# Normalizing the attention output after its repacking, two blocks at a time

## The chip, the cores and the metric

One core of a Trainium2 chip runs the whole computation. The metric is device time in microseconds of one execution. The engines of the core work side by side[...]: TensorE (PE, matrix products and their weight loads), ScalarE (ACT, activation functions), VectorE (DVE), GpSimd (POOL), and SyncE (SP), which here only issues DMAs. Products land in PSUM, eight banks of 128 partitions by 512 float32; everything else lies in SBUF.

## The reference

Two layers of the same kind, each an attention part and a mixer and MLP part, on x of 1 x 2048 x 512 in bfloat16:

```python
def _A_ref(x, wq, wk, wv, wo):                    # H = 32 heads, Dh = 16
    q = (x @ wq).reshape(B, S, H, Dh).transpose(0, 2, 1, 3)
    k, v = x @ wk, x @ wv                         # one key and value head for all
    p = _softmax(einsum("bhqd,bkd->bhqk", q, k) * Dh ** -0.5)
    return einsum("bhqk,bkd->bhqd", p, v).transpose(0, 2, 1, 3).reshape(B, S, H * Dh) @ wo

x = x + _A_ref(_layernorm(x), A_wq, A_wk, A_wv, A_wo)
x = x + _B_ref(_layernorm(x), B_w1, B_w2, B_w3, B_w4)
# and both once more
```

`_B_ref` is a gelu projection with shifts along the sequence (w1, w2) and a gelu MLP of width 1792 (w3, w4), each behind a layernorm. The attention has no mask. The softmax needs a division by the row sum of the exponentials; where that division takes place is what the change is about.

## The kernel before

**The planner.** The program is not written as an order of instructions. `Plan` holds operations, each with its engine, the tags it reads and writes, a priority (lower goes first) and a duration, and plays them through in a model of the engines. The order that comes out is emitted, one instruction stream for each engine, with semaphore waits where an operation depends on one of another engine. So a stream is fixed when the program is built: on the chip an engine takes its instructions in that order and waits when one is not yet allowed. Durations in the code (`dur=`) only shape the plan.

**Attention.** The 2048 queries are cut into chunks (`CHUNKS`): four of 512 in layer 0; three of 512 and two of 256 in layer 1. A block is four heads of a chunk, so a chunk has eight blocks, 72 in all. A block's keys are passed in steps of 128 (two steps at once in the chunks of 256), each step in two halves of two heads. There are 2048 such halves. Each half's exponential is made in one of two ways:

- a *unit* (`declare_unit`): scores on PE, one exponential of 128 x 1024 on ACT (L1125) into EA, one group of value products on PE (L1230);
- a *pair* (`declare_pair`): scores of each head on PE into a bank of its own, two DVE instructions (L1143) that turn them into the bit pattern of an approximate exponential in J, two shifted copies of it made by `shift_op` (L1180, on POOL, or on DVE when POOL's queue holds `ADDS` or more), and three groups of value products, with the value copies in VD that are scaled for the three.

Units are made in order. `assign` is asked whenever scores are placed and turns a half that lies ahead into a pair, when fewer than `MAX_PAIRS` pairs are in flight, when DVE's queue is short and when its due side work is below `BACKLOG`. In the stage between the layers (layer 1's first chunk, keys before step 11, which are ready early) these two numbers are replaced by `CALM`, and in the last chunk by `CALM_END`. `TEMPER` is a string of one letter for each 12.5 us of planned time, which picks one of 16 sets of the planner's numbers, `MAX_PAIRS` and `ADDS` among them.

Beside the attention of one chunk runs the side work of the chunk before: output projection, mixer, MLP, and for layer 1 its normalized input, keys and values. `PACE` and priorities hold it back or push it.

**Layer 1's first chunk** is special. Its last keys come from layer 0's last chunk, so seven of its blocks are first done for keys 0 to 5, then 6 to 10, with partial sums spilled in between, and finished later (`end == "add"`), in short blocks of five key steps.

**The end of a block** (`block_end`) is where the change is. The value products of four heads lie in one PSUM bank, `ACC`: head x on partitions 32x to 32x+15, the sums of its exponentials on partition 32x+16. Before the change the steps are, for a block of n queries:

1. DVE copies ACC to ACCF (L1264, or L1260 with the spilled part added). ACCF holds 1024 columns: two blocks of 512, or four of 256. The next block's products wait for this copy.
2. PE turns the sums into columns (SELC, L1274), DVE takes reciprocals into RZ (L1281).
3. PE spreads the reciprocals over 128 x n in a PSUM bank, with RZ columns as weights against the identity (`fx`, L1289).
4. DVE multiplies ACCF by it into OS (L1295).
5. SP issues eight DMAs (L1318) that repack OS into half of an OT tile: row 64 (b mod 2) onwards of tile b // 2, with no gaps between heads. In the last chunk of a layer, blocks of number `LATE_OT` and over are repacked by PE and DVE instead (SELO, L1308, L1314).

When all eight blocks of a chunk are through, `chunk_end` declares the output projection from OT (L676 with WO, OT) and the sum into X (L1450).

Of the kernel before, what the change touches and what calls it, by code (L numbers as in the profile page):

```python
# [10 lines left out]
ALU = mybir.AluOpType  # L11
# [498 lines left out]
def t_ps(n):  # L510
    return 0.066 + n * 1.043e-3
# [14 lines left out]
def tiled(n, k=1):  # L526
    return ("P", n * k, n * k, range(4))
# [6 lines left out]
class Kernel:  # L534
# [16 lines left out]
    PARTS = (0.3203125, 0.25390625, 0.201171875)  # L551
    FILL = True
    HOLD = 0.1
    CALM = (1, 1)
    CALM_END = (2, 1)
    LATE_OT = 5
    PORTION = 2
    QUICK = -1
    PACE = ((2.8, 2.8, 2.2, 0.3), (2.8, 2.2, 0.5, 0.5, None))
# [29 lines left out]
    )  # L589
    TEMPER = "090ee27f7f97f71e3eee4ee77f547c4fe941e77e7385715f85317197105502005897e0e10e0ef77f27f593f70f1f030e1e77ee0975325855000003"  # L590

    def __init__(self, nc, ins, out):
        self.stretch = -1
# [22 lines left out]
    def memory(self):  # L616
        self.sbytes = 0
        sb = self.sb
        self.X = sb("X", [16, 512])
        self.IDENT = sb("IDENT", [128])  # L620
        self.ONES = sb("ONES", [512])
        self.NIL = sb("NIL", [128])
        self.SELC = sb("SELC", [4])
        self.SELO = sb("SELO", [2, 32])
        self.WQ = sb("WQ", [4, 528])
        self.WK = sb("WK", [4, 32])
        self.WV = sb("WV", [4, 32])
        self.WO = sb("WO", [4, 512])
        self.W1 = sb("W1", [4, 512])
        self.W2 = sb("W2", [4, 512])  # L630
        self.W3 = sb("W3", [4, 1792])
        self.W4 = sb("W4", [14, 512])
        self.KT = sb("KT", [2, 2048])
        self.VP = sb("VP", [2, 16, 32])
        self.VD = sb("VD", [3, 2, 16, 32])
        self.QT = sb("QT", [2, 8, 512])
        self.OT = sb("OT", [4, 512])
        self.OS = sb("OS", [1024])
        self.QS = sb("QS", [4, 512])
# [12 lines left out]
        self.RZ = sb("RZ", [32])  # L652
        self.OUTB = sb("OUTB", [2, 512])
        self.ST6 = sb("ST6", [16, 6], dt.float32)
        self.MV = sb("MV", [16, 2], dt.float32)
        self.SM = sb("SM", [4, 16], dt.float32)
        self.MH = sb("MH", [2, 16], dt.float32)
        assert self.sbytes <= 208 * 1024, self.sbytes / 1024
        pb = self.stack.enter_context(self.nc.psum_tensor("PB", [128, 8, 512], dt.float32))
        self.PB = pb[:, :, :]  # L660
        self.PBH = self.shaped(pb[:].rearrange("p a b -> p (a b)").bitcast(dt.bfloat16), [8, 1024])
        kt0 = self.KT[:, 0, :].bitcast(dt.float32)
        ob = self.OUTB.rearrange("p a b -> p (a b)").bitcast(dt.float32)
# [46 lines left out]
    def head(self):  # L710
        pl = self.pl
        op = pl.op
        ins = self.ins
# [14 lines left out]
        def fill(eng, ap, v, tags, dur, prio):  # L728
            op(eng, lambda e: e.memset(ap, v), writes=tags, dur=dur, prio=prio)
# [36 lines left out]
        self.qproj(0, 0, prio=3, blocks=(1,), direct=True, after=[("KT", 0, 7)])  # L766
        self.qproj(0, 0, prio=3, blocks=range(2, 8), after=[("KT", 0, 7)])
        fill("POOL", self.SELC, 0.0, [("SELC",)], 0.1, 3)
        op("POOL", lambda e: e.affine_select(out=self.SELC, in_=self.SELC, compare_op=ALU.not_equal,
                                             fill=1.0, base=-16, pattern=[[-32, 4]],  # L770
                                             channel_multiplier=1),
# [247 lines left out]
    def make_groups(self):  # L1019
# [47 lines left out]
        self.pairs = []  # L1067
        self.adds = []
        self.fin_left = {}
        self.main_done = False  # L1070

    def inputs(self, g):
# [165 lines left out]
    def block_end(self, la, c, b, end):  # L1238
        op = self.pl.op
# [10 lines left out]
            return  # L1250
        n = self.size(la, c)
        nq = n // 128
        m = self.nfin % (1024 // n)
        self.nfin += 1
        parts = range(2 * m, 2 * m + 2) if n == 512 else (m,)
        am, zm, om = ([(x, i) for i in parts] for x in ("ACCF", "RZ", "OS"))
        acc, rz, osm = self.ACCF[:, m * n:m * n + n], self.RZ[:, 4 * nq * m:4 * nq * (m + 1)], self.OS[:, m * n:m * n + n]
        if end == "add":
            ap, tags = self.SPILL[b]
            self.last_copy = op("DVE", lambda e: e.tensor_tensor(  # L1260
# [2 lines left out]
        else:  # L1263
            self.last_copy = op("DVE", lambda e: e.tensor_copy(acc, self.PB[:, self.ACC, 0:n]),  # L1264
               writes=[("AC",)] + am, dur=t_ps(n), prio=0, side=False)
        fin = min(5, self.RUSH[la][c])
        L = Late()

        def fz(e):
# [8 lines left out]

        def frec(e):
            with self.nc.allow_low_precision("the reciprocals feed a bf16 matmul"):  # L1280
                return e.reciprocal(rz, self.PB[:, L.bank, 0:4 * nq])  # L1281
        op("DVE", frec, writes=[L] + zm, dur=0.17, prio=fin, give=L)
        M = Late()
        for h in range(nq // 2):
            def fx(e, h=h):
                ins = None
                for q in (2 * h, 2 * h + 1):
                    for g in range(4):
                        ins = e.matmul(self.PB[32 * g:32 * g + 32, M.bank, q * 128:(q + 1) * 128],  # L1289
                                       lhsT=rz[:, 4 * q + g:4 * q + g + 1].to_broadcast([128, 32]),  # L1290
                                       rhs=self.IDENT, start=True, stop=True, tile_position=(0, 32 * g))
                return ins
            op("PE", fx, reads=zm + [("ID",)], writes=[M], pe=("P", 256, 256, range(4)), prio=fin,
               take=M if h == 0 else None)
        op("DVE", lambda e: e.tensor_tensor(out=osm, in0=acc, in1=self.PB[:, M.bank, 0:n],  # L1295
                                            op=ALU.mult),
           reads=am, writes=[M] + om, dur=t_ps(n), prio=fin, give=M)
        r0 = 64 * (b % 2)
        hw = n // 2
        if c == len(self.CHUNKS[la]) - 1 and b >= self.LATE_OT:  # L1300
            N = Late()

            def fo(e):
                ins = None
                for u in range(2):
                    for p in range(2):
                        x = r0 + 32 * p
                        ins = e.matmul(self.PB[x:x + 32, N.bank, u * hw:u * hw + hw], lhsT=self.SELO[:, u, :],  # L1308
                                       rhs=osm[:, p * hw:p * hw + hw], start=True, stop=True,
                                       tile_position=(0, x), skip_group_check=True)  # L1310
                return ins
            op("PE", fo, reads=om + [("SELO", i, u) for i in range(2) for u in range(2)], writes=[N],
               pe=("P", 2 * hw, hw, (r0 // 32, r0 // 32 + 1)), prio=fin, take=N)
            op("DVE", lambda e: e.tensor_copy(self.OT[r0:r0 + 64, b // 2, 0:n], self.PB[r0:r0 + 64, N.bank, 0:n]),  # L1314
               writes=[N, ("OT", b)], dur=t_ps(n), prio=fin, give=N)
        else:
            op("SP", lambda e: [
                e.dma_start(self.OT[r0 + 16 * (2 * p + i):r0 + 16 * (2 * p + i) + 16, b // 2, u * hw:u * hw + hw],  # L1318
                            osm[32 * (2 * i + u):32 * (2 * i + u) + 16, p * hw:p * hw + hw])
                for p in range(2) for i in range(2) for u in range(2)],  # L1320
               reads=om, writes=[("OT", b)], dma=128 * n, parts=8, prio=fin)
        if end == "add" and b >= 3:
            self.qproj(1, 1, prio=11, blocks=(2 * b - 6, 2 * b - 5), direct=True)
            if b == self.SPILLED - 1:
# [2 lines left out]
        left.discard(b)  # L1327
        if not left:
            self.chunk_end(la, c)

    def temper(self, now):
        w = int(now / self.STRETCH)
# [307 lines left out]
```

## Time and profile before

| what | value |
|---|---|
| three runs | 1483.88, 1484.53, 1486.28 us; median 1484.53 |
| the profiled execution | 1481.02 us, span 1479.2 us |
| granted TensorE clock, mean | 0.999 |
| value copies to ACCF | 65 plain (49 of 512, 16 of 256), 7 with the spilled part |
| multiplies into OS | 72: 56 of 512 at 680 ns, 16 of 256 at 413 ns |
| reciprocals | 72: 248 ns (512), 199 ns (256) |
| OT casts of the matmul repack | 6: 687 ns (512), 424 ns (256) |
| OT DMAs | 424 of 8 KB, 1.8 us to landing, and 104 of 4 KB, 2.2 us |
| filler products (ONES, NIL) | 532 matmuls, 49 us |

The span is the time from the first to the last instruction that the profiler saw. A busy PE is not a PE at its peak, since its instructions overlap and their ends are modelled[...]. Waits name the instruction that released the waiting one. The chain of waits is followed back from the last instruction of the program: an engine with a large share of it sets the time.

### The profile page before, as it was taken

The numbers are of one execution on the slowest core, as the hardware profiler recorded it, in microseconds if no ns is written. First come the engines' busy times: TensorE is split into PE (matmuls) and PEld (weight loads), VectorE is DVE, ScalarE is ACT, GpSimd is POOL, SyncE is SP. The second block draws the span as 40 slices with busy tenths as digits, with TensorE's granted clock in tenths as the row PEclk, the third lists the DMA queues.
The fourth block names the chain that finished last, engine by engine and source line by source line (L and its number), as shares of the span: only waits on it lengthen the run. The fifth ranks groups of instructions, "written<-read, shape, count | busy, mean of one in ns | idle before, by whom it ended". The sixth has DMA issues, their size and how long they took to land.

```text
span 1479.2 us, 66152 instructions
## 1 busy us (share of the span) xinstructions
PE 1454.1 (98%) x30189; PEld 651.1 (44%) x30189; DVE 1285.0 (87%) x2304; ACT 1421.3 (96%) x1511; POOL 1146.2 (77%) x817
## 2 busy tenths in 40 slices
PE   9999999999999999999999999999999999999999
PEld 4443434444444444444344444444444445555555
DVE  8989999989999979887886799999889989888863
ACT  7999999999999999999999999999999999999962
POOL 2788888878889878797765588889678898888640
PEclk9999999999999999999999999999999999999999
DMA  6100100001000000100000000010000000000000
GB/s 216 29 6 6 21 6 6 5 6 20 7 4 6 6 4 7 20 5 2 3 2 3 3 8 12 5 21 5 10 18 8 4 6 7 13 19 11 6 14 25
DMA packets 32153, 21.71 MB, mean 15 GB/s; under 512 B 12672, under 2 KB 31360, under 8 KB 31872
## 3 DMA queue, kind: packets, MB, share of 16 engines
q1 hardware_dynamic: 31872, 17.47, 5.0%
q8 instruction: 236, 3.87, 1.1%
q14 instruction: 45, 0.37, 0.1%
HBM read 7.90 MB, written 2.10 MB: 7 GB/s over the span
## 4 chain that ended last, share of the span: by engine, by line
ACT 74%; PE 21%; DVE 3%; POOL 1%; issue 0%; DMA 0%; POOLq 0%
ACT EA L1125 69%; PE PB L676 7%; PE PB L1081 7%; PE PB L1230 6%; ACT G L1573 3%; ACT L1125 1%; DVE J L1143 1%; ACT GP L1493 1%; POOL J L1180 1%; ACT L1573 1%; ACT L1493 1%; PE PB L875 1%; DVE ST L791 0%; DVE G L1568 0%; PE PB L932 0%
## 5 line engine op out<-in xcount | busy, mean ns | idle before, releaser
L1125 ACT ACTIVATE EA<-PB 128x1024 bf16<-128x1024 f32 x1419 | 1305.2, 1169 | 11.3 <-PE PB L1081 5.3
L1180 POOL TENSOR_SCALAR J<-J 128x2048 uint16<-128x2048 uint16 (+1 forms) x556 | 1006.1, 1810 | 233.5 <-DVE J L1143 126.4
L1143 DVE TENSOR_SCALAR J<-PB 128x512 uint16<-128x512 f32 x1258 | 808.5, 682 | 84.3 <-PE PB L1081 79.0
L1081 PE MATMUL PB<-QT,KT 32*128 32x512 bf16 (+1 forms) x4608 | 606.0, 360 | 13.7 <-ACT EA L1125 5.7
L1230 PE MATMUL PB<-J,VD 128*32 128x256 bf16 (+1 forms) x8448 | 413.9, 265 | 2.1 <-POOL J L1180 0.8
L1230 PE MATMUL PB<-EA,VP 128*32 128x256 bf16 (+1 forms) x6400 | 350.8, 263 | 0.7 <-DVE KT L1242 0.4
L1081 PEld LDWEIGHTS PB<-QT,KT 32*128 32x128 bf16 x4608 | 162.7, 91 | 385.0 <-ACT EA L1125 316.6
L1230 PEld LDWEIGHTS PB<-J,VD 128*32 128x32 bf16 x8448 | 176.1, 95 | 176.0 <-issue 133.9
L1230 PEld LDWEIGHTS PB<-EA,VP 128*32 128x32 bf16 x6400 | 150.3, 95 | 114.0 <-issue 90.9
L676 PE MATMUL PB<-ZT,W 128*32 128x512 bf16 (+2 forms) x2816 | 171.1, 342 | 0.2
L676 PE MATMUL PB<-W,G 128*32 128x512 bf16 x1624 | 104.2, 381 | 0.6 <-ACT G L1573 0.6
L1180 DVE TENSOR_SCALAR J<-J 128x2048 uint16<-128x2048 uint16 (+1 forms) x107 | 78.9, 737 | 8.8 <-POOL J L1180 7.9
L1568 DVE CAST G<-PB 128x512 bf16<-128x512 f32 (+2 forms) x126 | 72.5, 582 | 13.5 <-PE PB L676 12.2
L676 PEld LDWEIGHTS PB<-ZT,W 128*32 128x32 bf16 x2816 | 63.6, 96 | 33.5 <-issue 21.3
L811 POOL TENSOR_TENSOR SM<-SM,MH 128x2 f32<-128x2 f32 (+1 forms) x69 | 49.6, 722 | 22.2 <-DVE SM L813 13.5
L1573 ACT ACTIVATE G<-G 128x1792 bf16<-128x1792 bf16 x29 | 47.0, 1685 | 15.4 <-DVE G L1568 15.3
L676 PEld LDWEIGHTS PB<-W,G 128*32 128x32 bf16 x1624 | 37.5, 96 | 39.1 <-issue 11.6
L1295 DVE TENSOR_TENSOR OS<-ACCF,PB 128x512 bf16<-128x512 bf16 (+1 forms) x72 | 44.7, 621 | 7.3 <-PE PB L1289 7.0
L676 PE MATMUL PB<-ONES,NIL 128*32 128x512 bf16 x532 | 49.1, 400 | 1.6 <-DVE J L1143 0.5
L791 DVE BATCH_NORM_STATS2 ST<-X 128x6 f32<-128x512 bf16 x64 | 43.1, 681 | 1.8 <-DMA X<-in_A_x_dram 1.3
L1549 POOL TENSOR_TENSOR X<-Y,X 128x512 bf16<-128x512 bf16 x32 | 38.6, 1218 | 6.3 <-DVE Y L1531 4.6
L1264 DVE CAST ACCF<-PB 128x512 bf16<-128x512 f32 (+1 forms) x65 | 40.0, 615 | 2.5 <-PE PB L1230 2.4
(103 smaller groups left out, 765.7 us busy)
## 6 DMA issues: line engine op xcount, KB each, us to landing
OT<-OS SPq DMA_DIRECT2D x424, 8.0 KB, 1.8
W<-in_B_w_dram SPq DMA_DIRECT2D x2, 1792.0 KB, 14.9
X<-in_A_x_dram SPq DMA_DIRECT2D x8, 256.0 KB, 4.7
QT<-QS SPq DMA_DIRECT2D x32, 64.0 KB, 2.4
out_dram<-OUTB SPq DMA_DIRECT2D x16, 128.0 KB, 1.7
OT<-OS SPq DMA_DIRECT2D x104, 4.0 KB, 2.2
W<-in_B_w_dram SPq DMA_DIRECT2D x2, 512.0 KB, 9.3
WQ<-in_A_wq_dram SPq DMA_DIRECT2D x1, 512.0 KB, 4.1
```

The lines of the kernel that those rows point to most:

```text
L676: ins = e.matmul(self.PB[32 * g:32 * g + 32, bank, 0:n], lhsT=lhsT[:, 32 * g:32 * g + 32], rhs=rhs, start=start, stop=stop, tile_position= ...
L791: op("DVE", lambda e, tb=tb: e.bn_stats(self.ST6[:, tb, :], src(tb)), reads=[tagf(tb)], writes=[("ST", tb)], dur=0.606, prio=prio)
L811: op("POOL", lambda e: e.tensor_tensor(out=out, in0=src, in1=self.MH[:, 0, a:b], op=ALU.pow), reads=tags + [("MH",)], writes=tg(r), dur=0. ...
L1081: ins = e.matmul(self.PB[:, bank, j * n:(j + 1) * n], lhsT=self.KT[32 * h:32 * h + 32, la, (kb + j) * 128:(kb + j + 1) * 128], rhs=self.QT ...
L1125: o = q.feeds = op("ACT", lambda e: e.activation(self.EA[:, ea, :, :], self.PB[:, b0:b0 + 2, :], ACTF.Exp, scale=0.25), writes=bk + [("EA" ...
L1143: o = op("DVE", lambda e, i=i, L=L: e.tensor_scalar(out=self.J[:, 3 * s, i * 512:(i + 1) * 512], in0=self.PB[:, L.bank, :], scalar1=128 * ...
L1180: o = self.pl.op(eng, lambda e: e.tensor_scalar(out=self.J[:, d, :], in0=self.J[:, f, :], scalar1=float(self.STEP), scalar2=1.0, op0=ALU.a ...
L1230: ins = e.matmul(self.PB[32 * x:32 * x + 32, self.ACC, p * hw:p * hw + hw], lhsT=v[:, la, kb + j, :], rhs=ap[:, i, j * w + u * hw:j * w + ...
L1264: self.last_copy = op("DVE", lambda e: e.tensor_copy(acc, self.PB[:, self.ACC, 0:n]), writes=[("AC",)] + am, dur=t_ps(n), prio=0, side=False)
L1295: op("DVE", lambda e: e.tensor_tensor(out=osm, in0=acc, in1=self.PB[:, M.bank, 0:n], op=ALU.mult), reads=am, writes=[M] + om, dur=t_ps(n), ...
L1568: op("DVE", lambda e, f=f, L=L: e.tensor_copy(self.G2[:, f, 0:n], self.PB[:, L.bank, 0:n]), writes=[L] + [(x, f, i) for x in ("G2", "GE") ...
L1573: op("ACT", lambda e, i=i: e.activation(self.G2[:, :, i * 128:(i + 1) * 128], self.G2[:, :, i * 128:(i + 1) * 128], ACTF.Gelu_apprx_tanh), ...
```

## The change

Of the five steps, the DMA repack now comes second: it takes the sums without division from ACCF to OT, right after step 1. The reciprocals go to RZ, which keeps those of all eight blocks of a chunk. When both blocks of an OT tile are through (`half_done`), `scale_pair` follows: POOL spreads the reciprocals of the two blocks, each over 16 columns, into RZE; PE spreads these over the queries into one PSUM bank, with rows that fit OT's packing; DVE multiplies the OT tile in place, once for two blocks. Late blocks keep the old way in `repack`, in place in ACCF; they are now 6 and 7, not 5 to 7. OS is gone. RZ is cleared once at the start. `CALM` goes from (1, 1) to (2, 1), so that two pairs can be in flight between the layers, and `TEMPER` has other letters in 89 of its 118 places.

```diff
@@ -551,9 +551,9 @@
     PARTS = (0.3203125, 0.25390625, 0.201171875)
     FILL = True
     HOLD = 0.1
-    CALM = (1, 1)
+    CALM = (2, 1)
     CALM_END = (2, 1)
-    LATE_OT = 5
+    LATE_OT = 6
     PORTION = 2
     QUICK = -1
     PACE = ((2.8, 2.8, 2.2, 0.3), (2.8, 2.2, 0.5, 0.5, None))
@@ -587,7 +587,7 @@
         (0.55, 3.0, 1.5, 3.0, 0.7, 1.2, 3, 6, 0.0),
         (0.57, 2.0, 1.0, 2.0, 0.45, 1.0, 3, 4, 0.0),
     )
-    TEMPER = "090ee27f7f97f71e3eee4ee77f547c4fe941e77e7385715f85317197105502005897e0e10e0ef77f27f593f70f1f030e1e77ee0975325855000003"
+    TEMPER = "090e357fe7f4ff7e0f7e2eeeff72790e3f75e5ff7145fe87e4c1e43707f90000548fe5eeef9f07ece7eeeff1f0ef9fefee4f897fe741eccccccccc"
 
     def __init__(self, nc, ins, out):
         self.stretch = -1
@@ -635,7 +635,6 @@
         self.VD = sb("VD", [3, 2, 16, 32])
         self.QT = sb("QT", [2, 8, 512])
         self.OT = sb("OT", [4, 512])
-        self.OS = sb("OS", [1024])
         self.QS = sb("QS", [4, 512])
         self.YT = sb("YT", [3, 4, 512])
         self.ZR = sb("ZR", [4, 512])
@@ -649,7 +648,8 @@
         self.G2E = [(self.EA[:, f // 2, f % 2, :], ("EA", f // 2)) for f in range(2 * self.N_EA)]
         self.G2E += [(spare[:, f * 512:(f + 1) * 512], ("J", 0, 0, 0)) for f in range(14 - 2 * self.N_EA)]
         self.ACCF = sb("ACCF", [1024])
-        self.RZ = sb("RZ", [32])
+        self.RZ = sb("RZ", [2, 8, 8])
+        self.RZE = sb("RZE", [16, 32])
         self.OUTB = sb("OUTB", [2, 512])
         self.ST6 = sb("ST6", [16, 6], dt.float32)
         self.MV = sb("MV", [16, 2], dt.float32)
@@ -766,6 +766,7 @@
         self.qproj(0, 0, prio=3, blocks=(1,), direct=True, after=[("KT", 0, 7)])
         self.qproj(0, 0, prio=3, blocks=range(2, 8), after=[("KT", 0, 7)])
         fill("POOL", self.SELC, 0.0, [("SELC",)], 0.1, 3)
+        fill("POOL", self.RZ, 0.0, [("RZ", b) for b in range(8)], 0.1, 3)
         op("POOL", lambda e: e.affine_select(out=self.SELC, in_=self.SELC, compare_op=ALU.not_equal,
                                              fill=1.0, base=-16, pattern=[[-32, 4]],
                                              channel_multiplier=1),
@@ -1067,6 +1068,7 @@
         self.pairs = []
         self.adds = []
         self.fin_left = {}
+        self.half_done = set()
         self.main_done = False
 
     def inputs(self, g):
@@ -1250,11 +1252,13 @@
             return
         n = self.size(la, c)
         nq = n // 128
+        hw = n // 2
+        r0 = 64 * (b % 2)
         m = self.nfin % (1024 // n)
         self.nfin += 1
         parts = range(2 * m, 2 * m + 2) if n == 512 else (m,)
-        am, zm, om = ([(x, i) for i in parts] for x in ("ACCF", "RZ", "OS"))
-        acc, rz, osm = self.ACCF[:, m * n:m * n + n], self.RZ[:, 4 * nq * m:4 * nq * (m + 1)], self.OS[:, m * n:m * n + n]
+        am = [("ACCF", i) for i in parts]
+        acc = self.ACCF[:, m * n:m * n + n]
         if end == "add":
             ap, tags = self.SPILL[b]
             self.last_copy = op("DVE", lambda e: e.tensor_tensor(
@@ -1264,6 +1268,13 @@
             self.last_copy = op("DVE", lambda e: e.tensor_copy(acc, self.PB[:, self.ACC, 0:n]),
                writes=[("AC",)] + am, dur=t_ps(n), prio=0, side=False)
         fin = min(5, self.RUSH[la][c])
+        late = c == len(self.CHUNKS[la]) - 1 and b >= self.LATE_OT
+        if not late:
+            op("SP", lambda e: [
+                e.dma_start(self.OT[r0 + 16 * (2 * p + i):r0 + 16 * (2 * p + i) + 16, b // 2, u * hw:u * hw + hw],
+                            acc[32 * (2 * i + u):32 * (2 * i + u) + 16, p * hw:p * hw + hw])
+                for p in range(2) for i in range(2) for u in range(2)],
+               reads=am, writes=[("OT", b)], dma=128 * n, parts=8, prio=fin)
         L = Late()
 
         def fz(e):
@@ -1278,47 +1289,16 @@
 
         def frec(e):
             with self.nc.allow_low_precision("the reciprocals feed a bf16 matmul"):
-                return e.reciprocal(rz, self.PB[:, L.bank, 0:4 * nq])
-        op("DVE", frec, writes=[L] + zm, dur=0.17, prio=fin, give=L)
+                return e.reciprocal(self.RZ[:, :, b, 0:2 * nq].rearrange("p i (q u) -> p q i u", u=2),
+                                    self.PB[:, L.bank, 0:4 * nq].rearrange("p (q i u) -> p q i u", i=2, u=2))
+        op("DVE", frec, writes=[L, ("RZ", b)], dur=0.17, prio=fin, give=L)
...
-        if c == len(self.CHUNKS[la]) - 1 and b >= self.LATE_OT:
...
+        if late:
+            self.repack(b, n, acc, am, fin)
         else:
-            op("SP", lambda e: [
-                e.dma_start(self.OT[r0 + 16 * (2 * p + i):r0 + 16 * (2 * p + i) + 16, b // 2, u * hw:u * hw + hw],
-                            osm[32 * (2 * i + u):32 * (2 * i + u) + 16, p * hw:p * hw + hw])
-                for p in range(2) for i in range(2) for u in range(2)],
-               reads=om, writes=[("OT", b)], dma=128 * n, parts=8, prio=fin)
+            key = (la, c, b // 2)
+            if key in self.half_done:
+                self.scale_pair(b // 2, n, fin)
+            self.half_done.add(key)
...
+    def scale_pair(self, k, n, fin):
+
+        op = self.pl.op
+        M = Late()
+        ns = n // 256
+        b0 = 2 * k
+
+        def fx(e):
+            ins = None
+            for u in range(2):
+                for s in range(ns):
+                    j = u * ns + s
+                    for g in range(4):
+                        z = 8 * (g // 2) + 2 * ((g % 2) * ns + s) + u
+                        ins = e.matmul(self.PB[32 * g:32 * g + 32, M.bank, j * 128:(j + 1) * 128], lhsT=self.RZE[:, z, :],
+                                       rhs=self.IDENT, start=True, stop=True, tile_position=(0, 32 * g))
+            return ins
+        op("POOL", lambda e: e.tensor_copy(
+            self.RZE.rearrange("p z (i d) -> p z i d", i=2),
+            self.RZ[:, :, b0:b0 + 2, :].rearrange("p i b z -> p (b z) i").unsqueeze(3).to_broadcast([128, 16, 2, 16])),
+           reads=[("RZ", b0), ("RZ", b0 + 1)], writes=[("RZE",)], dur=0.72, prio=fin, port=True)
+        op("PE", fx, reads=[("RZE",), ("ID",)], writes=[M], pe=tiled(n), prio=fin, take=M)
+        ot = self.OT[:, k, 0:n]
+        op("DVE", lambda e: e.tensor_tensor(out=ot, in0=ot, in1=self.PB[:, M.bank, 0:n], op=ALU.mult),
+           writes=[M, ("OT", b0), ("OT", b0 + 1)], dur=t_ps(n), prio=fin, give=M)
+
+    def repack(self, b, n, acc, am, fin):
+
+        op = self.pl.op
+        nq = n // 128
+        hw = n // 2
+        r0 = 64 * (b % 2)
+        M = Late()
+        for h in range(nq // 2):
+            def fx(e, h=h):
+                ins = None
+                for q in (2 * h, 2 * h + 1):
+                    for g in range(4):
+                        ins = e.matmul(self.PB[32 * g:32 * g + 32, M.bank, q * 128:(q + 1) * 128],
+                                       lhsT=self.RZ[:, g // 2, b, 2 * q + g % 2:2 * q + g % 2 + 1].to_broadcast([128, 32]),
+                                       rhs=self.IDENT, start=True, stop=True, tile_position=(0, 32 * g))
+                return ins
+            op("PE", fx, reads=[("RZ", b), ("ID",)], writes=[M], pe=("P", 256, 256, range(4)), prio=fin,
+               take=M if h == 0 else None)
+        op("DVE", lambda e: e.tensor_tensor(out=acc, in0=acc, in1=self.PB[:, M.bank, 0:n], op=ALU.mult),
+           writes=[M] + am, dur=t_ps(n), prio=fin, give=M)
...
```

What is left out of `repack` at its end is the selection product and the OT cast of the old late path, word for word, with `acc` in the place of `osm`.

More of the change, by code (lines that the diff above doesn't have):

```diff
@@ L1280, in frec @@
             with self.nc.allow_low_precision("the reciprocals feed a bf16 matmul"):
-                return e.reciprocal(rz, self.PB[:, L.bank, 0:4 * nq])
-        op("DVE", frec, writes=[L] + zm, dur=0.17, prio=fin, give=L)
[L1283 to L1299, printed above, removed]
-        if c == len(self.CHUNKS[la]) - 1 and b >= self.LATE_OT:
[L1301 to L1315, printed above, removed]
-        else:
-            op("SP", lambda e: [
-                e.dma_start(self.OT[r0 + 16 * (2 * p + i):r0 + 16 * (2 * p + i) + 16, b // 2, u * hw:u * hw + hw],
-                            osm[32 * (2 * i + u):32 * (2 * i + u) + 16, p * hw:p * hw + hw])
-                for p in range(2) for i in range(2) for u in range(2)],
-               reads=om, writes=[("OT", b)], dma=128 * n, parts=8, prio=fin)
@@ new lines, in repack, with fo @@
+    def repack(self, b, n, acc, am, fin):
[17 more added lines that the diff above has]
+           writes=[M] + am, dur=t_ps(n), prio=fin, give=M)
+        N = Late()
+        def fo(e):
+            ins = None
+            for u in range(2):
+                for p in range(2):
+                    x = r0 + 32 * p
+                    ins = e.matmul(self.PB[x:x + 32, N.bank, u * hw:u * hw + hw], lhsT=self.SELO[:, u, :],
+                                   rhs=acc[:, p * hw:p * hw + hw], start=True, stop=True,
+                                   tile_position=(0, x), skip_group_check=True)
+            return ins
+        op("PE", fo, reads=am + [("SELO", i, u) for i in range(2) for u in range(2)], writes=[N],
+           pe=("P", 2 * hw, hw, (r0 // 32, r0 // 32 + 1)), prio=fin, take=N)
+        op("DVE", lambda e: e.tensor_copy(self.OT[r0:r0 + 64, b // 2, 0:n], self.PB[r0:r0 + 64, N.bank, 0:n]),
+           writes=[N, ("OT", b)], dur=t_ps(n), prio=fin, give=N)
```

## The prediction

> **What bounds the kernel now.** I read the page's engine shares and the chain of waits first, then the costliest groups, then equal 37 us windows, then the waits of single engines. Engine shares and chain, from the page:
>
> ```profile
> PE 1454.1 (98%) x30189; PEld 651.1 (44%) x30189; DVE 1285.0 (87%) x2304; ACT 1421.3 (96%) x1511; POOL 1146.2 (77%) x817
> ...
> ACT 74%; PE 21%; DVE 3%; POOL 1%; issue 0%; DMA 0%; POOLq 0%
> ```
>
> ScalarE (ACT) carries three quarters of the chain, TensorE (PE) a fifth. PE's 98% holds filler matmuls and pipelined ends, so the chain is the better witness: PE sets the pace in stretches, ACT elsewhere. The groups say what ACT does and what its rival path costs (columns: line, engine, operation, tiles, count, then busy us and mean ns):
>
> ```profile
> L1125 ACT ACTIVATE EA<-PB 128x1024 bf16<-128x1024 f32 x1419 | 1305.2, 1169 | 11.3 <-PE PB L1081 5.3
> L1180 POOL TENSOR_SCALAR J<-J 128x2048 uint16<-128x2048 uint16 (+1 forms) x556 | 1006.1, 1810 | 233.5 <-DVE J L1143 126.4
> L1143 DVE TENSOR_SCALAR J<-PB 128x512 uint16<-128x512 f32 x1258 | 808.5, 682 | 84.3 <-PE PB L1081 79.0
> ```
>
> The attention has 2048 half steps: 1419 go through ACT's exponential ("units", 1305.2 / 1419 = 0.92 us each), and 1258 / 2 = 629 through the integer trick on DVE and POOL ("pairs"). So time is gained by whatever lets the planner turn units into pairs: each one relieves ACT of 0.92 us. A pair costs DVE 2 x 0.682, plus 78.9 / 629 = 0.125 for its share of the shifts that run on DVE, plus 79.0 / 629 = 0.126 of waiting for scores: 1.62 us. On PE it costs two more value products. One four-way group of products costs 0.11 us: in the chain near the end, sixteen matmuls of L1230 take 0.34 us and thirty-two 0.56, so eight narrow ones (one product) 0.11. A score pass streams 512 columns, like one four-way group of the projections; 152 matmuls of L676 at 1425.29 take 8.38 us, 0.22 a group. A pair's two heads pass singly, so at most one such pass more: a pair costs PE 0.22 to 0.44 us more than a unit (estimated).
>
> Where each engine is short shows in the windows (start:end, length, then busy us of PE, weight load, DVE, ACT, POOL):
>
> ```profile
> 111.00:148.00 37.00, 35.68 (x652) 14.66 (x653) 33.56 (x57) 37.00 (x42) 31.29 (x17) 1.00 0.03 6
> ...
> 518.00:555.00 37.00, 36.44 (x720) 15.76 (x712) 28.82 (x55) 36.94 (x38) 27.79 (x25) 1.00 0.02 4
> ...
> 777.00:814.00 37.00, 36.23 (x662) 15.50 (x662) 25.08 (x46) 35.75 (x36) 21.83 (x15) 1.00 0.01 3
> ```
>
> In 111:148, pure attention, ACT has no idle time and DVE is 91% busy: DVE is what stops more pairs. In 518:555 (MLP beside attention) DVE idles 8 us and still few pairs are made: PE is full of projections. In 777:814, between the layers, DVE idles 12 us and POOL 15, and the chain runs through PE from 763 to 823 us in many pieces. DVE is busy 33 us or more in 22 of the 38 windows between the first and the last.
>
> **The change, part by part.**
>
> **DVE work removed.** The groups by form:
>
> ```profile
> L1295 DVE TENSOR_TENSOR OS<-ACCF,PB 128x512 bf16<-128x512 bf16 x56 | 38.1, 680 | 5.2 <-PE PB L1289 4.9
> L1289 PE MATMUL PB<-IDENT,RZ 128*32 128x128 bf16 x1024 | 29.7, 219 | 0.0
> L1464 POOL TENSOR_SCALAR ZR<-Y,SM 128x512 bf16<-128x512 bf16 x32 | 23.7, 750 | 1.8 <-POOL SM L811 0.5
> ```
>
> Four blocks (6 and 7 of both last chunks) keep their own multiply. The other 68 form 34 pairs of blocks, 27 of 512 queries and 7 of 256; each loses one multiply: 27 x 0.680 + 7 x 0.413 = 21.3 us. Block 5 of both last chunks goes from the matmul repack to DMA: two OT casts less, 0.69 + 0.42 = 1.1. Together 22.4 us of DVE. The reciprocal keeps its 16 elements and only writes them in strides: 0.25 us as before.
>
> **PE work removed.** The spreading matmuls fall from 1024 to 27 x 16 + 7 x 8 + 48 = 536. By the 0.22 us for sixteen such matmuls read above, 488 / 16 x 0.22 = 6.7 us. The selection product of two blocks goes too, under 0.5 us.
>
> **POOL work added.** 34 copies that spread the reciprocals over 512 elements. No such copy is in the trace; nearest is the one-input 512-element ZR row, median 0.70 us (0.69 to 1.12); the two-input row L1549, median 1.16, is the upper bound, and 0.27 us (the 8-element GP copies) the lower. I take 0.70: 34 x 0.70 = 24 us (9 to 39). POOL idles 333 us. Cover: it waits 126 us for DVE's J and 66 us for DVE's shifts.
>
> A rule speaks against this. The Trainium skill, "GPSIMD Engine Reference", section "Engine selection", sends elementwise work to VectorE, with one-input work about as fast on either. DVE's own 512-element one-input rows (L828) have medians near 0.41 us: there the copies would cost 34 x 0.41 = 14 us and leave 8 of the 22 us, a gain under 3 us. The rows say POOL is the idle engine, so I weigh its slower 0.70 as cheap. But POOL runs in order: a shift queued behind a spread is late by 0.70, and PE's next products of J wait for it. In the waits by line, PE waited for a POOL or DVE shift 83 times over 663 shifts, 12.5%; so 34 x 0.125 x 0.70 = 3 us of PE, half of it beside ACT work: 1.5 us lost (0 to 24, if every spread delayed everything).
>
> The second rule: "SBUF — State Buffer", section "Who interferes with whom", has one port pair, held exclusively by a GpSimd instruction or a two-port VectorE instruction. The trace agrees in kind: the DVE shift has median 0.68 and maximum 1.88 us, ZR on POOL median 0.70, maximum 1.12. DVE's two-port rows (L1180 79 us, L828 55 us) fill 9% of the span; 34 x 0.09 x 0.7 is 2 us at most if every meeting costs a whole copy, half that by the mean. I put 0.5 us into the same margin.
>
> **DMA moved.** Repacking DMAs (eight per block, 8.0 KB, 1.8 us to landing, issue about 0.6 to 0.73 each) now start from ACCF right after the accumulator copy, not after the multiply. There are 68 x 8 = 544 instead of 528. On SP only the QT moves and at the end the output stores stand beside them; early on QT's (from 40.96 and 63.00, 5 us each) and OT's (52.90, 72.03) stay clear of each other. New wait: the accumulator copy two blocks later needs that ACCF half back, and behind it on DVE stand the pair casts and on PE the next block's products. Blocks are normally about 21 us apart (182.24 and 203.56): cover of over 30 us against 5.8 + 1.8 = 7.6. At the layer's first chunk short blocks come quickly (L1260 at 874.46, 879.29, 884.74): two apart is 10.3 us, less 0.7 for the copy leaves 9.6, so 2 us of cover. I take 0; if it is gone, up to 2 us for each of five blocks, +10. After a chunk's end the first new block's DMA waits for the output projection, which in the trace is over by 207 us while that ACCF half is needed near 246. The scale multiply waits for the later of DMA and spread; nothing but the output projection needs it.
>
> **Pair limit between the layers** (CALM). It allows two pairs in flight instead of one while layer 1's first chunk waits for its last keys. The windows from 740 to 851 have 28 us of idle DVE, so up to 28 / 1.62 = 17 more pairs: ACT -16 us. PE pays 17 x 0.22 to 0.44 = 4 to 7 us, just where the chain is PE's, and DVE's spare time feeds the MLP and normalization that make the last keys. Bounds -4 (ACT only ever waited 4.6 us there) and +12; the nearest row, the PE-bound window, says no gain: 0.
>
> **The planner's moods** (TEMPER) change in most of their 12.5 us stretches. No row prices this. Half a pair per window, one-sided, over 38 windows would be 19 x 0.92 = 17 us; by chance signs some 3. I take 0, and -8 to +8 for the range.
>
> **Sum.** Only in the 22 of 38 windows where DVE is short does its relief turn into pairs: 0.58 x 22.4 = 13.0 us. A converted pair spends 1.62 us and shortens the stage by 0.92, in which DVE would have worked 0.9 of the time: x = 13.0 / (1.62 + 0.83) = 5.3 pairs, so ACT and the span lose 5.3 x 0.92 = 4.9 us. In the other 16 windows PE's relief counts: 0.42 x 6.7 = 2.8 us. Less 1.5 for POOL: -6.2 us. The profiled execution took 1481.0 us (span 1479.2 and 1.8 around it), so 1474.8 there. The runs' median, 1484.5, is 3.5 higher: **1478 us**.
>
> **Rivals.** (A) The forecast, 1470 to 1481.4: chance 0.45. (B) It pays twice: the freed DVE time converts everywhere (22.4 / 2.45 x 0.92 = 8.4) and PE's 6.7 counts in full: -15 us, 1469, with good moods 1462. For it: DVE idles in every window anyway, so buffers may not be the limit. Against: 518:555. Chance 0.10. (C) Nothing arrives: the repacked path was hidden, freed DVE time becomes more waiting for scores (79 us already), 1482 to 1487. For it: PE at 98%. Chance 0.12. (D) Slower: between the layers the added pairs make PE and DVE late with the MLP, layer 1's keys 11 to 15 come late, and ACT starves. Seventeen pairs cost PE 7 us, and 28 us of DVE work ahead of the side chain delay it by up to half, 14: +21, less the 6 gained elsewhere: +15, 1499; from about 8 added pairs (10 us of delay against 6 gained) it decides. For it: the PE chain at 763 to 823 and ACT's first idle time there. Against: planned side work goes first when its DVE backlog is over 1 us. Chance 0.33.
>
> A measurement of this kernel can tell about 0.2% (3 us) from no change. Faster 0.55, same 0.12, slower 0.33. The range 1465 to 1496 holds A, C, most of B and the lower two thirds of D. The likeliest case's own range is 1470 to 1481.
>
> **What would show it.** Right: multiplies on DVE fall from 72 to 38, a POOL copy to RZE appears 34 times near 0.70 us, casts of L1143's kind rise from 1258 to about 1270, exponentials fall to about 1413, DVE waits for ACCF stay under 1 us. Wrong: exponentials unchanged (C); ACT idle over 10 us between 740 and 870 with more casts there (D); POOL copies of over 1.1 us or PE waiting for POOL's J well above 20 us; the accumulator copy waiting for DMA.

## The result and the profile after

The changed kernel takes 1472.12 us (median of 6 runs, 1471.57 to 1472.26), the kernel before 1483.89 (6 runs, 1481.19 to 1486.28): a ratio of 0.9922 with a 95% interval of 0.991 to 0.9935. That is 11.8 us less. The profiled execution has a span of 1470.2 us, 9.0 less than before.

The engine shares and the chain of waits, from the page of the changed kernel:

```profile
PE 1446.2 (98%) x29813; PEld 646.8 (44%) x29813; DVE 1295.5 (88%) x2323; ACT 1406.4 (96%) x1496; POOL 1140.3 (78%) x830
...
ACT 73%; PE 22%; DVE 3%; POOL 2%; issue 0%; POOLq 0%
```

The kind of bound is the same: ACT three quarters, PE a fifth. ACT has 14.9 us less to do: 12.3 us of exponentials, and 2.6 us because it loads a function table 30 times instead of 32, at 1.28 us each. The span fell by 9.0 of that, since ACT's idle time grew by 5.9. DVE, which lost multiplies, is *busier* by 10.5 us. Where that went is in the groups (the exponentials, the shifts on POOL, the casts of the pairs, the shifts on DVE; same columns as before):

```profile
L1127 ACT ACTIVATE EA<-PB 128x1024 bf16<-128x1024 f32 x1406 | 1292.9, 1172 | 12.3 <-PE PB L1083 6.1
L1182 POOL TENSOR_SCALAR J<-J 128x2048 uint16<-128x2048 uint16 (+1 forms) x534 | 976.6, 1829 | 213.9 <-DVE J L1182 90.1
L1145 DVE TENSOR_SCALAR J<-PB 128x512 uint16<-128x512 f32 x1284 | 821.8, 681 | 81.6 <-PE PB L1083 77.5
...
L1182 DVE TENSOR_SCALAR J<-J 128x2048 uint16<-128x2048 uint16 (+1 forms) x136 | 98.6, 725 | 7.2 <-POOL J L1182 6.5
```

Thirteen halves went over from units (1419 to 1406) to pairs (1258 to 1284 casts). On DVE that is 13.3 us more for casts and 19.7 us more for shifts (107 before, 136 now), against 21.3 us less for multiplies and 1.2 for OT casts: +10.5. POOL runs 22 shifts fewer and makes the spreads instead. The new operations, by form:

```profile
L1328 POOL COPY RZE<-RZ 128x512 bf16<-128x512 bf16 x34 | 22.4, 658 | 4.0 <-DVE RZ L1292 1.6 <-DVE Y L829 0.4 <-DVE J L1145 0.2
...
L1334 DVE TENSOR_TENSOR OT<-OT,PB 128x512 bf16<-128x512 bf16 x27 | 18.3, 677 | 0.0
...
L1325 PE MATMUL PB<-IDENT,RZE 128*32 128x128 bf16 x488 | 12.8, 220 | 0.0
...
L1334 DVE TENSOR_TENSOR OT<-OT,PB 128x256 bf16<-128x256 bf16 x7 | 2.9, 412 | 0.1
```

The spreads are 34 at 0.66 us, and no multiply ever kept DVE waiting (the 0.0 and 0.1 behind the bar).

The gain is not even along the run. The time of the copy to ACCF that ends each chunk's attention, from the DVE timelines (us; the last columns are explained below):

| chunk ends | before | after | undone_last_chunk | undone_layer_1 |
|---|---|---|---|---|
| layer 0, first | 182.2 | 181.1 | 180.6 | 180.6 |
| second | 351.5 | 350.4 | 349.9 | 349.9 |
| third | 520.7 | 526.2 | 525.8 | 525.7 |
| fourth | 704.0 | 691.5 | 691.0 | 691.0 |
| layer 1, first | 905.9 | 899.3 | 898.9 | 906.0 |
| second | 1076.0 | 1066.8 | 1066.4 | 1077.2 |
| third | 1242.0 | 1234.8 | 1234.2 | 1254.0 |
| fourth | 1331.4 | 1326.4 | 1325.1 | 1355.9 |
| fifth | 1421.8 | 1410.7 | 1417.9 | 1444.3 |

After two chunks the changed kernel is 1 us ahead, after three 5.5 behind, after four 12.5 ahead; the stage between the layers gives 6 back. Were 0.7 us of DVE time per pair of blocks simply turned into pairs, the lead would grow by about a microsecond per chunk.

Most of this swing is work that moved, not time that was won. ACT also runs the gelus of the MLP (L1573 before, L1615 after), and the new plan puts them into other chunks. With their table loads they take nothing instead of 15.5 us in the fourth chunk, and 7.7 us more than before both in the third chunk and in the stage between the layers. With the moved gelus taken out, the lead is 2.2 us after three chunks, 4.8 after four and 6.6 after the stage.

Where halves went over from units to pairs, by stretch (before, after; an instruction that runs across a boundary counts on both sides):

| stretch | exponentials | pair casts | ACT idle, us |
|---|---|---|---|
| layer 0 (to 704.0; to 691.5) | 702, 701 | 653, 658 | 12.4, 10.8 |
| between the layers (to 905.9; to 899.3) | 196, 187 | 132, 149 | 4.7, 9.9 |
| behind it | 523, 521 | 474, 478 | 40.8, 43.0 |

Nine of the thirteen exponentials went in the stage between the layers, where the pair limit is now two. Its lines, exponentials first and casts second, each before and after (start:end, length, busy us, count):

```profile
704.00:905.90 201.90, 179.43 (x196) 1.00 0.02 5
691.50:899.30 207.80, 171.09 (x187) 1.00 0.02 5
704.00:905.90 201.90, 85.84 (x132) 1.00 0.02 5
691.50:899.30 207.80, 96.27 (x149) 1.00 0.02 5
```

That is 8.3 us less of exponentials, and 5.2 us more of idle time on ACT take most of it back. The windows in which ACT idles and after it (PE, weight load, DVE, ACT, POOL):

```profile
740.00:777.00 37.00, 36.56 (x797) 18.02 (x790) 32.02 (x68) 28.19 (x29) 16.11 (x20) 1.00 0.01 3
777.00:814.00 37.00, 36.93 (x729) 16.94 (x721) 29.33 (x56) 36.03 (x39) 22.77 (x17) 1.00 0.01 3
```

and ACT's timeline inside the first of them:

```profile
761.55 6.52 ACT L1127 ACTIVATE EA<-PB 128x1024 bf16<-128x1024 f32 x7 [5.14 <-PE PB L1232]
768.09 1.28 ACT L1615 ACT_TABLE_LOAD   x1
772.99 3.29 ACT L1615 ACTIVATE G<-G 128x1792 bf16<-128x1792 bf16 x2 [3.62 <-DVE G L1610]
```

ACT stands still for 5.1 and 3.6 us while PE is full. Before the change it did 35.57 us of work in this window:

```profile
740.00:777.00 37.00, 36.50 (x700) 15.51 (x698) 30.56 (x63) 35.57 (x38) 23.92 (x23) 1.00 0.01 2
```

Only 6 pair casts fall in it, 16 before; the added pairs come later (58 casts between 777 and 851 us, 40 before).

### The profile page after: what moved, and what is told of

Same layout as the page of the kernel before. It is cut to its first block, busy times and chain, and to the rows that moved or that the text cites. A ratio compares the mean times of both kernels' runs of the same rounds, so it can differ in the third digit from the quotient of the medians.

```text
span 1470.2 us, 65395 instructions
## 1 busy us (share of the span) xinstructions
PE 1446.2 (98%) x29813; PEld 646.8 (44%) x29813; DVE 1295.5 (88%) x2323; ACT 1406.4 (96%) x1496; POOL 1140.3 (78%) x830
## 4 chain that ended last, share of the span: by engine, by line
ACT 73%; PE 22%; DVE 3%; POOL 2%; issue 0%; POOLq 0%
ACT EA L1127 68%; PE PB L676 8%; PE PB L1083 6%; PE PB L1232 6%; ACT G L1615 2%; POOL J L1182 1%; ACT L1127 1%; DVE J L1145 1%; ACT GP L1535 1%; PE PB L876 1%; ACT L1535 1%; ACT L1615 1%; DVE G L1610 0%; PE PB L933 0%; DVE J L1182 0%
## 5 line engine op out<-in xcount | busy, mean ns | idle before, releaser
L1127 ACT ACTIVATE EA<-PB 128x1024 bf16<-128x1024 f32 x1406 | 1292.9, 1172 | 12.3 <-PE PB L1083 6.1
L1182 POOL TENSOR_SCALAR J<-J 128x2048 uint16<-128x2048 uint16 (+1 forms) x534 | 976.6, 1829 | 213.9 <-DVE J L1182 90.1
L1145 DVE TENSOR_SCALAR J<-PB 128x512 uint16<-128x512 f32 x1284 | 821.8, 681 | 81.6 <-PE PB L1083 77.5
L1232 PE MATMUL PB<-J,VD 128*32 128x256 bf16 (+1 forms) x8628 | 418.5, 265 | 3.0 <-POOL J L1182 1.1
L1232 PE MATMUL PB<-EA,VP 128*32 128x256 bf16 (+1 forms) x6340 | 343.8, 263 | 1.0 <-DVE QT L1244 0.3
L1182 DVE TENSOR_SCALAR J<-J 128x2048 uint16<-128x2048 uint16 (+1 forms) x136 | 98.6, 725 | 7.2 <-POOL J L1182 6.5
L812 POOL TENSOR_TENSOR SM<-SM,MH 128x2 f32<-128x2 f32 (+1 forms) x69 | 50.7, 735 | 22.0 <-DVE SM L814 13.3
L1615 ACT ACTIVATE G<-G 128x1792 bf16<-128x1792 bf16 x29 | 47.0, 1686 | 19.5 <-DVE G L1610 19.4
L814 POOL TENSOR_SCALAR SM<-MV 128x2 f32<-128x2 f32 (+1 forms) x45 | 12.3, 272 | 31.6 <-DVE MV L794 29.7
```

What stands on the lines that cost most here:

```text
L812: op("POOL", lambda e: e.tensor_tensor(out=out, in0=src, in1=self.MH[:, 0, a:b], op=ALU.pow), reads=tags + [("MH",)], writes=tg(r), dur=0. ...
L1127: o = q.feeds = op("ACT", lambda e: e.activation(self.EA[:, ea, :, :], self.PB[:, b0:b0 + 2, :], ACTF.Exp, scale=0.25), writes=bk + [("EA" ...
L1145: o = op("DVE", lambda e, i=i, L=L: e.tensor_scalar(out=self.J[:, 3 * s, i * 512:(i + 1) * 512], in0=self.PB[:, L.bank, :], scalar1=128 * ...
L1182: o = self.pl.op(eng, lambda e: e.tensor_scalar(out=self.J[:, d, :], in0=self.J[:, f, :], scalar1=float(self.STEP), scalar2=1.0, op0=ALU.a ...
L1232: ins = e.matmul(self.PB[32 * x:32 * x + 32, self.ACC, p * hw:p * hw + hw], lhsT=v[:, la, kb + j, :], rhs=ap[:, i, j * w + u * hw:j * w + ...
L1615: op("ACT", lambda e, i=i: e.activation(self.G2[:, :, i * 128:(i + 1) * 128], self.G2[:, :, i * 128:(i + 1) * 128], ACTF.Gelu_apprx_tanh), ...
```

## The experiments

### Block end and moods, each without the other

`struct_only` is the changed kernel with the limit and string of before; `moods_only` is the reverse.

```diff
 # struct_only, from the changed kernel
-    CALM = (2, 1)
+    CALM = (1, 1)
-    TEMPER = "090e357fe7f4ff7e..."
+    TEMPER = "090ee27f7f97f71e..."
 # moods_only: the same two edits the other way, from the kernel before
```

> The changed block end alone: the new repacking and scaling (and blocks 6, 7 late), with the pair limit and the moods of the kernel before. Theory 'structure' (the freed DVE time is turned into pairs by whatever moods): 1472 to 1480 us, exponentials at most 1413. Theory 'moods' (the gain lies in the new letters and the new limit): 1483 or more, exponentials near 1419. A third reading, that a mood string is fitted to one plan and is worth nothing on another: clearly over 1490.

> The old block end with the new moods and the new pair limit. Theory 'structure': not faster than before, 1484 or more. Theory 'moods': 1472 to 1478 with some 1406 exponentials. 'Fitted to one plan': over 1490.

Measured: `struct_only` 1557.7 us (ratio to before 1.05, 1.0484 to 1.0516), `moods_only` 1541.24 (1.0394, 1.0378 to 1.0409). Each half of the change alone makes the kernel slower by some 4 or 5%; the third reading holds. What ACT waited for in `struct_only` (us in total, times, longest):

```profile
ACT EA L1127 <- PE PB L1232: 35.6, 16, 5.5
ACT EA L1127 <- PE PB L1083: 23.3, 11, 10.9
```

Before the change these two waits were 5.3 us each. The plan leaves ACT starved for 59 us, and its exponentials are 1434, not fewer.

### One mood everywhere

```diff
-    TEMPER = "090e..."
+    TEMPER = "000000..."        # flat_old, flat_new; "cccccc..." in uniform_c_old, uniform_c_new
-    CALM = (2, 1)               # in the two with the new block end
+    CALM = (1, 1)
```

> The kernel before with the same mood (letter 0) in every stretch: a plan that no string was fitted to. It serves as the base for flat_new. 'Fitted' expects it 10 us or more above the kernel before; 'structure' has no say on its height.

> The changed block end with letter 0 in every stretch and the old pair limit, so that only the block end differs from flat_old. Theory 'structure': 6 to 12 us below flat_old, with 7 to 14 fewer exponentials. Theory 'moods': within 3 us of flat_old.

Measured: `flat_old` 1539.48 us (1539.32 to 1541.11), `flat_new` 1533.29 (1533.17 to 1534.79). The new block end is 6.2 us faster with nine exponentials fewer, as the theory 'structure' forecast. One pair of plans can agree by chance, though, so a second:

> The kernel before with letter c in every stretch (as letter 0, but up to five shifts may queue on GpSimd instead of four). A second plan that no string was fitted to, as the base for uniform_c_new: about 1525 to 1545 us, as flat_old.

> The changed block end with letter c in every stretch and the old pair limit, so that only the block end differs from uniform_c_old. If the 6.2 us of the flat pair are what the block end is worth on any plan: 3 to 9 us below uniform_c_old. If a new plan moves the time by more than the block end does, and the flat pair was one draw of that: outside this band, and the other sign is possible (3 us or more above uniform_c_old).

Measured: `uniform_c_old` 1521.28 us (1521.03 to 1521.78), `uniform_c_new` 1532.77 (1532.39 to 1533.0): now 11.5 us *slower*. The exponentials and pair casts of the two, from their pages, old block end first:

```profile
L1125 ACT ACTIVATE EA<-PB 128x1024 bf16<-128x1024 f32 x1453 | 1336.5, 1174 | 17.5 <-PE PB L1230 11.9
...
L1143 DVE TENSOR_SCALAR J<-PB 128x512 uint16<-128x512 f32 x1190 | 768.4, 683 | 149.0 <-PE PB L1081 146.2
```

```profile
L1127 ACT ACTIVATE EA<-PB 128x1024 bf16<-128x1024 f32 x1454 | 1337.5, 1150 | 19.2 <-PE PB L1232 10.2
...
L1145 DVE TENSOR_SCALAR J<-PB 128x512 uint16<-128x512 f32 x1188 | 767.8, 683 | 170.3 <-PE PB L1083 166.5
```

The last part of each line is to be read: DVE's idle time before the casts grew by 21 us, about the 22 us that the change took off DVE. Not one exponential went over to a pair. What grew most on ACT is another wait, for DVE's casts of the gelu's input (old block end first; us in total, times, longest):

```profile
ACT G L1573 <- DVE G L1568: 16.4, 2, 13.0
ACT G L1615 <- DVE G L1610: 27.1, 5, 13.3
```

That is 10.7 us more, where the profiled span grew by 11.1. So the block end alone gave -6 us in one neutral plan and +12 in the other: what it is worth depends on the plan around it. Put on the other block end, the strings of before and after (1558 and 1541 us) do no better than one letter everywhere (1533 us twice with the new block end; 1521 and 1539 with the old).

### DVE time in a fixed order

The two runs here, and the two on the spread below, keep every order and wait of a kernel and change only what one instruction does; the planner isn't told.

```diff
 # old_quarter_multiply, from the kernel before (OS cleared once at the start)
-        op("DVE", lambda e: e.tensor_tensor(out=osm, in0=acc, in1=self.PB[:, M.bank, 0:n],
+        op("DVE", lambda e: e.tensor_tensor(out=osm[:, 0:n // 4], in0=acc[:, 0:n // 4], in1=self.PB[:, M.bank, 0:n // 4],
 # new_extra_multiply, from the changed kernel
+            e.tensor_tensor(out=self.SPARE2[:, 0:n], in0=ot, in1=self.PB[:, M.bank, 0:n], op=ALU.mult)
             return e.tensor_tensor(out=ot, in0=ot, in1=self.PB[:, M.bank, 0:n], op=ALU.mult)
```

> The kernel before with its own plan, order and waits, but each multiply into OS covers a quarter of its columns (the rest of the attention output stays zero): about 56 x 0.40 + 16 x 0.2 = 25 us of DVE time less, what the change takes off, and not one exponential moved to another engine. Theory 'relief counts where it falls' (a fixed order already gains from a freer DVE): 1472 to 1478. Theory 'relief counts only through the plan' (DVE's idle time just grows): within 3 us of the kernel before.

> The changed kernel with its own plan and order; each of the 34 scalings multiplies twice, the first time into a spare tile: 27 x 0.68 + 7 x 0.41 = 21 us of DVE time more, unplanned. 'Relief counts where it falls': 6 to 12 us slower than the changed kernel (1478 to 1484). 'Only through the plan': 1472 to 1475.

`old_quarter_multiply`: 1481.61 us, ratio to before 0.9996 (0.9986 to 1.0005). 25.6 us less of multiplies bought nothing that can be told from the scatter (DVE's busy time, which counts overlapping instructions once, fell by 20.3):

```profile
L1143 DVE TENSOR_SCALAR J<-PB 128x512 uint16<-128x512 f32 x1258 | 809.7, 683 | 101.4 <-PE PB L1081 96.5
...
L1295 DVE TENSOR_TENSOR OS<-ACCF,PB 128x128 bf16<-128x128 bf16 (+1 forms) x72 | 19.1, 265 | 7.3 <-PE PB L1289 7.0
```

The multiplies fell from 44.7 to 19.1 us, and DVE's waiting for scores rose from 79.0 to 96.5. In this order the relief turned into waiting.

`new_extra_multiply`: 1479.52 us, ratio to before 0.9982 (0.997 to 0.9993), some 7 us above the changed kernel. Here the first theory holds: added time costs, though removed time did not pay. The chain of waits of that run:

```profile
ACT 45%; PE 41%; DVE 9%; POOL 3%; issue 1%; DMA 0%; DVEq 0%; POOLq 0%
```

DVE and PE now hold half of the chain, against a quarter in the changed kernel. The plan had too little slack on DVE to absorb an unplanned 21.2 us of multiplies (14.5 us of busy time); a third of it came through. The two runs change two different plans, so they don't show what relief would do to the new plan or a load to the old one.

### The price of the spread on GpSimd

```diff
 # new_no_spread (RZE cleared once at the start)
-            self.RZE.rearrange("p z (i d) -> p z i d", i=2),
-            self.RZ[:, :, b0:b0 + 2, :].rearrange("p i b z -> p (b z) i").unsqueeze(3).to_broadcast([128, 16, 2, 16])),
+            self.RZE[:, 0, 0:8], self.RZ[:, 0, b0, 0:8]),
 # new_double_spread: the same copy first into a spare tile, then into RZE
+            e.tensor_copy(self.SPARE2.rearrange("p z (i d) -> p z i d", i=2), src)
```

> The changed kernel with its own plan, where GpSimd copies 8 elements instead of 512 (the attention output is left scaled by zeros): 34 x about 0.4 = 14 us of GpSimd time less. If the spread costs the 1.5 us that the prediction put on it: 1470 to 1472. If it blocks the shifts behind it: 1465 or less.

> The changed kernel with its own plan; GpSimd makes each spread twice (once into a spare tile): 22 us of GpSimd time more. By the prediction's price (1.5 us for 24 us on GpSimd): 1473 to 1475. If GpSimd's order is tight: over 1480.

`new_no_spread`: 1470.88 us, ratio 0.9916 (0.9901 to 0.9931), which overlaps the changed kernel's; its copies took 8.1 us in place of 22.4. `new_double_spread`: 1478.61, ratio 0.997 (0.9959 to 0.9982), about 6.5 us above the changed kernel, more than the prediction's price and less than the tight reading. The planned spread is nearly free; an unplanned one costs 0.19 us of its 0.66. This is the same one-sidedness as on DVE, here within one plan.

### Undoing the block end in the late part only

Both start from the changed kernel and keep its string and limit. In the chunks named in OLD a block is scaled by itself in ACCF before its DMA, the order of before (but without OS).

```diff
+    OLD = ((1, 4),)                              # undone_last_chunk
+    OLD = tuple((1, c) for c in range(5))        # undone_layer_1
+        old = (la, c) in self.OLD
-        if not late:
+        if not late and not old:
             op("SP", lambda e: [ ... ])           # DMA of ACCF, unscaled
...
+        elif old:                                # spread and multiply in ACCF, then the same DMA
+            self.scale_block(b, n, acc, am, fin)
```

> The changed kernel, but in the last chunk of layer 1 alone blocks are scaled one by one in ACCF before the DMA, as before the change; up to there the plan is the changed kernel's. By the count of DVE time, three multiplies of 0.41 us come back, about 1.2 us, and no spread on GpSimd: within 2 us of the changed kernel, 1470 to 1474. By the fit (every plan change costs the letters behind it): slower by more than 4 us, 1476 or more.

> The changed kernel up to the end of layer 0's attention; in layer 1 blocks are scaled one by one in ACCF before the DMA. By the count of DVE time, 12 x 0.68 + 7 x 0.41 = 11 us of DVE come back, half of the forecast gain: 3 to 6 us slower, 1475 to 1478. By the fit: 15 us or more slower, over 1487, with layer 0 ending at the same times as in the changed kernel (its eighth blocks' copies at 181, 350, 526 and 691 us).

`undone_last_chunk`: 1478.77 us, ratio to before 0.9975 (0.9965 to 0.9985), so 6.7 us above the changed kernel for three multiplies worth 1.2. `undone_layer_1`: 1502.8, ratio 1.0139 (1.0121 to 1.0157), 31 us above it for 11 us of DVE time. The table of chunk ends shows both as the changed kernel up to the first undone chunk, and the loss growing from chunk to chunk behind it: in `undone_layer_1` 7, 10, 19, 29, 34 us. Its ACT starves:

```profile
ACT EA L1128 <- PE PB L1233: 24.4, 12, 5.1
```

In the changed kernel that wait is 5.8 us. ACCF, which these two hold until the DMA is through, isn't the reason: in `undone_layer_1` its plain copies waited 2.0 us, all of it for PE. The reading that fits is that the letters suit one plan, and from the first difference on they are letters for another. How they were chosen is not known here.

## Why the prediction was right or wrong

The sign and the range were right, the size half: -6.2 us forecast, -11.8 measured (-9.0 between the two profiled spans). By its steps:

- **The bound** held. ACT's work is what counts, and the way to less of it is more pairs: 13 units fewer took 12.3 us off ACT. Two things that stand in no term of the sum came with it: 2.6 us less of table loads and 5.9 us more of idle time.
- **DVE and PE work removed**: the counts were exact (38 multiplies, 536 spreading matmuls), and so were DVE's sums, 21.3 us of multiplies and 1.2 of casts.
- **POOL**: 0.70 us was taken for the spread, 0.66 measured. Its price of 1.5 us fits `new_no_spread` (1.2 us gained for 14 us less). Its in-order blocking stayed small: PE's products waited for the spread itself for 1.1 us in all. The copies took 0.61 us at the median and 1.14 at most; whether the shared port stretched the long ones is not shown.
- **DMA moved and the ACCF wait**: taken at 0, measured at 0. In the short blocks of layer 1's first chunk the copies that share a half of ACCF follow each other by 12 to 14 us in the new trace, and DVE never stood idle before them (the 0.0 in the first line). The plain copies waited for PE alone:

```profile
L1264 DVE TENSOR_TENSOR ACCF<-PB,QT 128x512 bf16<-128x512 f32 x4 | 2.7, 679 | 0.0
...
its engine sat idle before it (us, times) until:
  PE PB L1232: 3.4, 9
```

- **The pair limit between the layers** was taken at 0, with rival D at its side. The stage made 8.5 pairs more: 8.3 us less of exponentials against 5.2 us more of idle time on ACT, some -3 us. So most of the added pairs are where the forecast put none. D's sign was nearly met (ACT idle for 9.8 us between 740 and 870, 4.7 before, with 86 casts instead of 78). But the idle time lies where casts were fewer, not more, and without the moved gelus the lead grew in this stage. A row that was read for D was also read too widely: before the change the chain ran through PE from 763.5 to 767.5 and from 800.0 to 823.4 us, and through ACT between. The new limit was not tried alone, so how much of this is the limit's and how much the letters' is open.
- **The conversion of DVE relief into pairs** (13.0 us into 5.3 pairs) is the step that the runs do not bear out. It assumed that a freer DVE gets more pairs by itself. In a fixed order it gets none (`old_quarter_multiply`). Planned anew, it got nine in one plan and none in another (`flat_new`, `uniform_c_new`). In the changed kernel 4.5 pairs were gained outside the stage between the layers, near the 5.3, but no run shows that DVE's relief made them. The match of 6.2 us with the flat pair is one draw. Rival C, where freed DVE time becomes waiting for scores, describes these two runs, `old_quarter_multiply` and `uniform_c_new`, though not the changed kernel.
- **The moods**, "I take 0, and -8 to +8 for the range", is a term that was mis-sized. The same block end takes 1472 us with its own letters and limit and 1558 with those of before: 86 us. "By chance signs some 3" was the scatter expected of a new plan; the two uniform pairs gave -6.2 and +11.5.

That the total fell within its range is in part luck: the terms taken at 0, limit and letters, moved the time by more than the whole forecast. The gain is shown for block end, limit and letters together, as one plan; how it divides among them stays open. The later start of the late blocks (`LATE_OT`) went with the block end in every run and was not tried alone. Whether letters fitted equally hard to the old block end would reach 1472 was not measured. No run here that computes the whole result is faster than the changed kernel.

## What to carry to other kernels

When a program builds its own order from a model and its parameters were chosen for one order, price a change of structure and a change of the parameters as one thing: here neither had a worth of its own, and undoing a part cost far more than the work that came back. To learn what an operation costs, keep the order and change only that instruction; to learn what its removal could be worth, plan it anew at several neutral settings, since one pair can agree with a forecast by chance. Where a table by stage shows a swing, count first what work changed its stage. And ask of every freed microsecond which queue will use it: in the fixed order tried here it turned into waiting.

## What the runs showed of the hardware

In the fixed orders tried, time was one-sided on two engines. Taking 25.6 us of multiplies off DVE in the old plan changed the kernel's time by less than could be told (0.9996); adding 21.2 us of them in the new plan cost some 7. In the new plan, taking 14 us off GpSimd gave about 1, and adding the spreads once more (22.4 us in the changed kernel) cost 6.5. GpSimd's 512-element copy with a broadcast source ran at a median of 0.61 us (0.61 to 1.14), faster than its one-input arithmetic on 512 plain elements (median 0.69), and in a third of the time of a 2048-element shift (1.90 mean).
